# Expert layers: the low parts of the weights subtracted by VectorE a step later, instead of by GpSimd

## The chip, the cores and the metric

The kernel runs on 1 core of one Trainium2 chip. The metric is device time in microseconds (us) of one execution, the median of several. Five engines work side by side, each through its own queue in order: TensorE (PE, with PEld for its weight loads), VectorE (DVE), ScalarE (ACT), GpSimd (POOL) and SyncE (SP, which here only issues DMAs).

## The reference

Three layers follow one another: attention that keeps the 32 largest scores of a row, a mixture of 8 experts with a fixed capacity of 288 tokens each, and one more MLP with h * cos(h).

```python
def _moe_ref(x, w_gate, w1, w2):            # x [2304, 512]
    logits = x @ w_gate
    order = np.argsort(-logits.flatten())
    ...                                     # greedy: each token to the best expert that is not full
    for e in range(E):                      # E = 8, w1 [512, 1024], w2 [1024, 512] each
        mask = assigned == e
        h = np.maximum(x[mask] @ w1[e], 0.0)
        out[mask] = h @ w2[e]
    return out.astype(np.float32)
```

The MLP behind it computes `h = x @ w_in; (h * cos(h)) @ w_out`, with weights in float64.

## The kernel before

Attention takes the first 500 us of the span, the experts the stretch from 533 to 863 us, the last MLP the rest.

**Products in two parts.** A float32 operand is split into a high part `a0 = Copy(a)` in TensorE's reduced format (written `F32R`) and a low part `a1 = a - a0`. A product is three passes: high x high, high x low, low x high. The weights come from DRAM in units of 128 x 1024 (512 KB): SP loads a unit into one of three buffers `raw` (`fetch`, L1056), ACT copies it into the high half of a tile `wu` (L1070), and one subtraction writes the low half (`split`, L1073 where it is issued at once, L1252 where it was put off). A buffer `raw` is free for the next load when both have read it.

**The loop over the experts** (`m1`) has 64 steps (expert e, eighth f) and two more to drain. A step i does, in the order of the program: the subtractions that were put off in the step before; `h` of step i (12 matmuls, L1170, the result cut at 0 and split by ACT at L1176 and DVE at L1177 into `hh`); a tick of the search; `y` of step i - 2 (12 matmuls, L1185); another tick; the split of the next unit or units of weights by `more`; and one or two instructions of the float64 conversion `conv` on DVE (L1106 to L1121). Each engine keeps this order; nothing is scheduled again.

**The search** (`Search`, called by `tick`) assigns the tokens to the experts beside these matmuls. It plays between two engines: DVE compares all tokens with 24 thresholds (`v` by L795, then the table `yh` by L756), TensorE counts (L784), DVE judges (L788, L789), TensorE spreads the answer (L791), and so on, four rounds an expert. `place` then works out the rows of one expert's tokens (L844 to L881 on DVE, L851 and L869 on TensorE), and GpSimd gathers them by indirect DMAs (L1147). The first step begins when the first expert is known. From step 5 on, `i + 7` units of weights have been split at the end of step i; an expert takes 8 units and 8 steps, and the last unit of its first layer is split two steps before that expert's first `h`.

**Put off or not.** `split` appends the subtraction to the list `late` where it is given both an engine and that list; the loop issues what is in `late` at the start of the next step, and fetches the next unit after that. Without an engine the subtraction goes to GpSimd at once:

```python
            low = partial((eng or nc.gpsimd).tensor_tensor, w[:, 1, :], raw, w[:, 0, :].bitcast(F32), op=OP.subtract)
            if eng is None or late is None:
                low()
            else:
                late.append(low)
```

Of the kernel before, what the change touches and what calls it, by code (L numbers as in the profile page):

```python
# [19 lines left out]
DRAM = bass.MemoryType.DRAM  # L20

EPS1 = 1.0 - 2.0 ** -24          # the float32 next below 1
BIG = 2e37
NB = 64                          # thresholds that a round of the routing's search tries
NS, NR = 24, 4                   # the same where logits are without ties, and the rounds
MAGIC = 1.5 * 2.0 ** 23
INV2PI = 1.0 / (2.0 * math.pi)
C1 = 6.28125                     # 2 pi = C1 + C2, k * C1 exact
C2 = 2.0 * math.pi - 6.28125
PASSES = ((0, 0), (0, 1), (1, 0))  # high x high, high x low, low x high  # L30

B, H, S, D = 4, 8, 576, 64
NP = B * H // 2                  # pairs of heads
# [7 lines left out]
def constants(k, tmp):  # L41
# [24 lines left out]
    # token of (partition, column): 4 columns of a batch's first 512, then the last 64 of two batches each  # L66
# [34 lines left out]


WARM = 6, 4                       # products that keep the tensor engine's clock up: at the start, and when the scores end
LAST = 8                          # so many last tiles have their exp masked by the vector engine alone
PLACES = 3                        # places of a pair's q and k
MID = 8                           # in the first steps of the experts the search has two ticks more
CI, CR = 8, 5                     # from this step on, so many quarters of an instruction of the float64 weights a step
NY = 6                            # places of stretches of y
L2 = 3                            # steps from a second layer's h to its o


class Attention:
    """Scores of 128 queries at a time (tile): two heads of a pair by 4 tiles each, and one tile of both heads' last 64."""
# [3 lines left out]
    def __init__(s, k, sb, ps, slow=False):  # L117
# [4 lines left out]
        # their places are taken again only by weights  # L122
# [27 lines left out]
    def load(s, p):  # L150
        """k and q with the head dimension on partitions; q's pair of heads apart, zeros beside each"""
# [21 lines left out]
    def qk_mm(s, j, c):  # L173
        # even tiles have the last 64 keys last, odd ones first
        p, hs, i = s.tiles[j]
        if c == 0:
            s.SP[j] = s.ps.tile([128, 2, 512], F32, name="sp", bufs=s.nsp)
        o = 64 if j % 2 == 0 else 0
        lh = s.QT[p][hs][:, i * 128:(i + 1) * 128] if hs < 2 else s.QT[p][2]
        s.nc.tensor.matmul(s.SP[j][:, c, :288], lh, s.KT[p][:, o + c * 288:o + c * 288 + 288], start=True, stop=True)  # L180
# [34 lines left out]
    def sign_exp(s, j):  # L215
        # sign(t(1-e) - s(1-e)): -1 from t on, 1 below, never 0 (t no power of 2); the sum gives the count
# [31 lines left out]
    def probs(s, j, kind):  # L248
        """exp of the kept scores; by 'a' with a minus where not kept, which the copy after the transposition drops"""
# [89 lines left out]
    @staticmethod  # L339
    def together(*gens):  # L340
        """a step of each in turn: the words of one have time to arrive while another works"""
        gens = list(gens)
        while gens:
            gens = [g for g in gens if next(g, gens) is not gens]

    def store(s, b):
        """x of a batch to DRAM"""
# [5 lines left out]
    def logits_t(s):  # L353
        """a finished pair's part of x, transposed"""
# [14 lines left out]
    def logits_m(s):  # L369
        """and its share of the logits"""  # L370
# [18 lines left out]
    def span(s):  # L389
        """from the logits of the first three batches: a range wider by a half, of which a 24th is the search's first step;  # L390
        and what is far below it"""
# [26 lines left out]
    def warm(s, n):  # L418
        """keeps the tensor engine's clock up where it would wait for long"""
        for i in range(n):  # L420
            w = s.ps.tile([128, 2, 512], F32, name="sp", bufs=s.nsp)
            s.nc.tensor.matmul(w[:, 0, :], s.wt[:, :128], s.wt, start=True, stop=True)

    def run(s):
# [9 lines left out]
        # a pair is loaded in the step after the last scores of the one whose place it takes  # L434
# [3 lines left out]
        for step in range(ng + 6):  # L438
            gA, gB, gC, gD, gE, gF, gG = [step - i for i in range(7)]
            # when the scores are through, what is left goes on without a step between  # L440
# [74 lines left out]
    def run_slow(s):  # L515
        """any scores: 32 largest by 4 rounds of 8"""
        nc, sb = s.nc, s.sb
        V, A = nc.vector, nc.scalar
        for j, (p, hs, i) in enumerate(s.tiles):
# [35 lines left out]
            # v and q, k of a pair are needed until the last tile of the pair's group is done: NV = 2  # L555


def attention_flag(k, big):
    """where a row's 32nd largest was not proven: count out of 24..31, t or T tiny, negative or a power of 2"""
# [13 lines left out]
class Routing:  # L573
    """Pairs (token, expert) in descending logit: a token gets the first expert that is not full. In a phase all open
    experts take tokens down to the threshold at which the first of them is full; 64 thresholds a round find it."""
# [4 lines left out]
    def start(s):  # L580
        k, nc, sb, ps = s.k, s.nc, s.sb, s.ps
        PEe, V, A, G = nc.tensor, nc.vector, nc.scalar, nc.gpsimd
        # these few words lie apart, where no store has to end first
# [25 lines left out]
    def counts(s, m, O, th):  # L609
        """[E, NB]: the tokens from each threshold on, by best expert"""  # L610
# [9 lines left out]
    def over(s, pc):  # L620
        """[128, NB]: how many experts would overflow if all tokens from a threshold on were taken"""
# [6 lines left out]
    def take(s, m, O, G1):  # L628
        """assigns the tokens with G1 to their best experts; closes experts that are full"""
# [19 lines left out]
    def run_slow(s):  # L649
        """any logits: a token's ties by expert, the search down to neighbouring floats, ties between tokens by place"""  # L650
# [13 lines left out]
        with tc.For_i(0, E, 1):  # L664
# [7 lines left out]
            # hi: nothing is above; lo: all that is left is at or above  # L672
# [22 lines left out]
            # from hi on all; the ties in [lo, hi) as far as there is room, by place  # L695
# [24 lines left out]
class Search:  # L720
    """The same for logits without ties, beside other work: tick() is called where the tensor engine has time for a few
    products. Thresholds lie evenly over the logits' range; NS of them, NS between two of these, and so on for NR rounds
    find the one at which the first expert is full. The experts are numbered in this order, and
    each one's tokens are known as soon as it is full."""
# [8 lines left out]
    def tick(s, n=9):  # L733
        # first what the tensor engine does for all of them
# [17 lines left out]
    def compare(s, v):  # L752
        """[v >= -t] for t from 1 to NS"""
# [5 lines left out]
    def search(s):  # L759
# [7 lines left out]
        for r in range(E):  # L767
# [8 lines left out]
            else:  # L776
# [5 lines left out]
                for z in range(NR):  # L782
# [3 lines left out]
                    # thresholds at which no expert would take too many  # L786
# [34 lines left out]
            # which one was full: 16 + its number, if it was one  # L821
# [12 lines left out]
    def place(s, r, A, new):  # L834
        """the rows of x of the tokens of the expert that is number r"""
# [40 lines left out]
        # and these tokens' places among all  # L876
# [8 lines left out]
    def finish(s):  # L885
        """the rows of the output by place, 128 a block; and whether all was proven"""
# [34 lines left out]
def verdict(k, p):  # L921
    """k.bad: 1 if anything was not proven. Every expert has exactly its 288, and each was the only one full in its turn"""
# [3 lines left out]
    if p is not None:  # L926
        nc.tensor.matmul(p, k.onesf, u, start=True, stop=True)
        V.tensor_scalar(k.bad, p[:1], 0.0, None, op0=OP.is_gt)
        # if so, rows that are all different
# [13 lines left out]
def prefix(k, Ab, pp):  # L943
    """pp[p, c, e]: tokens before (p, c) with Ab, by columns"""
# [7 lines left out]
def slots(k, sb, ps):  # L952
    """the tokens sorted by expert, as row numbers for the gathers (96 a block) and the stores (128 a block)"""
# [47 lines left out]
class FFN:  # L1001
    """Both MLPs with the features on partitions. A float32 operand is split exactly into two parts of 12 bits."""
# [3 lines left out]
    def __init__(s, k, rt=None):  # L1006
# [3 lines left out]
        # units of weights in the order of their splitting: those of the first expert and of the next one's first layer;  # L1010
        # then, while expert e is in work, w1 of the next and w2 as its places get free
# [10 lines left out]
    def own(s, w, e, lo, hi):  # L1022
        """rows of an expert's weights"""
# [4 lines left out]
    def ready(s, half=False):  # L1028
        """are the next unit's (or half's) numbers float32, by an instruction issued before?"""
# [5 lines left out]
    def fetch(s, n, half=False):  # L1035
        """the next n units (or halves) of weights as they are"""
# [21 lines left out]
    def split(s, n, half=False, eng=None, late=None):  # L1058
        """the next n units (or halves) into high and low parts"""
# [17 lines left out]
    def narrow(s, lo, hi, tiles, temp):  # L1077
        """float64 weights to float32, rounded, half a unit at a time: yields between instructions"""
# [20 lines left out]
        for n in range(lo, hi):  # L1099
# [5 lines left out]
            # sign and exponent's top bit; 7 bits of exponent and 20 of mantissa  # L1105
# [11 lines left out]
            # the other 32 bits of mantissa, in units of the number's power of 2  # L1117
# [4 lines left out]
            # below float32's smallest normal: 0, or is there any? the high word as a float32 is in order, too  # L1122
# [18 lines left out]
    def gather(s, e):  # L1141
        """x of an expert's tokens"""
# [7 lines left out]
    def m1(s, sb, ps, yT):  # L1150
# [57 lines left out]
        def more(n, eng=None):  # L1208
            """n units have been split by now"""
# [40 lines left out]
        for i in range(len(seq) + LAG):  # L1250
# [18 lines left out]
            if i < len(seq):  # L1269
# [10 lines left out]
                if (e, f) == (E - 1, 4):  # L1280
                    # the tables of the second half
                    A.activation(s.sin, s.half_pi, AF.Sin)
            if rt:
                more(i + 5 + (i >= 2) + (i >= 5), eng=V if i >= 61 or i in (1, 3) else None)
# [14 lines left out]
    def part(s, k, c):  # L1299
        """y of stretch k's tokens in two parts"""  # L1300
# [7 lines left out]
    # stretch, half of the weights, its eighth; is it the stretch's first or last?  # L1308
# [17 lines left out]
    def turns(s, i, q):  # L1326
        # cos h = sin(pi/2 - |h - 2 pi k|)
# [212 lines left out]
```

## Time and profile before

| what | value |
|---|---|
| time, median of 3 runs | 1322.13 us |
| lowest and highest run | 1317.45 and 1332.7 us |
| span of the profiled execution | 1308.3 us |
| mean granted TensorE clock over the span | 0.926 |
| busy shares of the span, PE / DVE / ACT / POOL | 89% / 85% / 60% / 58% |

The span runs from the first to the last instruction of the profiled execution. Its own time with what lies around the span is not given apart; the median of the runs is 13.8 us above its span, the lowest run 9.2 us. The stretches of the program are told apart by windows of the span, in us from its start.

### The profile page before, as it was taken

The page shows a single profiled execution, that of the slowest core. Times are in us where ns is not written, and L with a number is a line of the kernel's source. Part 1 is how long each engine was busy: PE and PEld are TensorE (multiplying, and loading weights), DVE is VectorE, ACT ScalarE, POOL GpSimd, SP SyncE. Part 2 cuts the span into 40 slices and gives each one's busy share as a digit, 9 for nine tenths or more (in the row PEclk, how much of TensorE's full clock was granted, in tenths as well). Part 3 has the DMA queues.
Part 4 walks back from the last instruction along what each step waited for, and adds up shares of the span by engine and source line. Part 5 has one row for each costly group of instructions (what it writes and reads, how often), then busy time and mean ns, then how long its engine had stood idle before and what let it go on. Part 6 is the DMA issues. An engine that isn't in the chain of part 4 may idle for free.

```text
span 1308.3 us, 22623 instructions
## 1 busy us (share of the span) xinstructions
PE 1170.2 (89%) x7449; PEld 1036.4 (79%) x7449; DVE 1115.0 (85%) x4001; ACT 784.0 (60%) x1503; POOL 758.2 (58%) x655
## 2 busy tenths in 40 slices
PE   6799999999899995768878888998899999999996
PEld 3677787788777785668878888997778899999995
DVE  7999999999999995776697789979999767777774
ACT  7989888889898871323334344655565545444442
POOL 5988887889887870554545466745574434211120
PEclk9989898899898897878798888999899899999998
DMA  4201121111110001444454555642332101000000
GB/s 118 54 22 43 32 66 30 31 61 36 30 30 37 2 1 69 154 124 156 122 163 147 163 162 164 210 138 73 110 116 81 57 1 42 25 25 25 26 25 28
DMA packets 61888, 98.06 MB, mean 75 GB/s; under 512 B 30912, under 2 KB 30912, under 8 KB 61248
## 3 DMA queue, kind: packets, MB, share of 16 engines
q1 hardware_dynamic: 53648, 74.47, 18.8%
q10 hardware_dynamic: 5136, 12.60, 2.7%
q0 software_dynamic: 2976, 9.44, 2.3%
q8 instruction: 61, 1.00, 0.3%
q14 instruction: 67, 0.55, 0.1%
HBM read 78.66 MB, written 17.83 MB: 74 GB/s over the span
## 4 chain that ended last, share of the span: by engine, by line
DVE 51%; PE 40%; issue 4%; ACT 1%; POOL 1%; DMA 1%; SPq 0%; DVEq 0%; POOLq 0%; ACTq 0%
PE pa L1322 10%; PE y L1370 9%; DVE C L190 8%; PE pa L1170 5%; PE y L1185 5%; PE av L303 3%; DVE w L238 3%; DVE P L257 2%; PE sp L180 2%; DVE ct L1330 2%; PE pa L869 2%; DVE C L205 2%; DVE w L233 2%; DVE w L235 1%; DVE r L1121 1%
## 5 line engine op out<-in xcount | busy, mean ns | idle before, releaser
L1322 PE MATMUL pa<-yh,wu 128*128 128x384 f32 x1152 | 224.3, 342 | 9.5 <-POOL yh L1306 4.9
L1370 PE MATMUL y<-wu,gh 128*128 128x512 f32 x864 | 222.0, 401 | 6.6 <-POOL gh L1358 6.1
L1322 PEld LDWEIGHTS pa<-yh,wu 128*128 128x128 f32 x1152 | 207.7, 191 | 21.0 <-POOL yh L1306 6.3
L226 POOL TENSOR_TENSOR W<-sg,S 128x576 f32<-128x576 bf16 x144 | 195.8, 1367 | 47.3 <-ACT sg L220 46.6
L1073 POOL TENSOR_TENSOR wu<-raw,wu 128x1024 fp32r<-128x1024 f32 x63 | 157.2, 2508 | 108.0 <-ACT wu L1070 99.8
L1370 PEld LDWEIGHTS y<-wu,gh 128*128 128x128 f32 x864 | 164.1, 192 | 39.8 <-POOL gh L1358 8.0
L180 PE MATMUL sp<-kT,qz 128*128 128x288 f32 x512 | 174.9, 432 | 9.6 <-ACT S L184 7.2
L303 PE MATMUL av<-vm,PT 128*128 128x65 f32 (+1 forms) x1216 | 153.4, 275 | 30.1 <-DVE xb L326 29.7
L303 PEld LDWEIGHTS av<-vm,PT 128*128 128x128 f32 (+1 forms) x1216 | 141.7, 191 | 38.1 <-DVE xb L326 35.4
L190 DVE MAX8 C<-S 128x8 f32<-128x72 f32 x1152 | 162.5, 215 | 5.6 <-ACT S L184 5.4
L264 POOL TENSOR_TENSOR P<-sg,E 128x576 f32<-128x576 bf16 x102 | 135.8, 1332 | 3.6
L1170 PE MATMUL pa<-xh,wu 128*128 128x288 f32 x768 | 132.1, 326 | 6.2 <-DVE hh L1177 3.8
L1354 ACT ACTIVATE gh<-cx 128x384 fp32r<-128x384 f32 x95 | 49.9, 525 | 145.1 <-DVE cx L1352 143.8
L1170 PEld LDWEIGHTS pa<-xh,wu 128*128 128x128 f32 x768 | 118.4, 212 | 13.1 <-issue 4.7
L1185 PE MATMUL y<-hh,wu 128*128 128x288 f32 x768 | 127.5, 319 | 0.0
L184 ACT ACTIVATE S<-sp 128x576 f32<-128x576 f32 x144 | 95.1, 660 | 53.2 <-PE sp L180 53.2
L272 PEld LDWEIGHTS pt<-ident,P 128*128 128x128 f32 x576 | 82.0, 148 | 52.7 <-POOL P L264 8.3
L1185 PEld LDWEIGHTS y<-hh,wu 128*128 128x128 f32 x768 | 116.8, 208 | 2.6 <-ACT r L1129 1.8
L272 PE MATMUL pt<-ident,P 128*128 128x128 f32 x576 | 112.8, 284 | 4.4 <-POOL P L264 2.0
L220 ACT ACTIVATE sg<-S,tb 128x576 bf16<-128x576 f32 x144 | 114.5, 795 | 2.7 <-DVE tb L211 2.7
L222 ACT ACTIVATE E<-S,nmx 128x576 f32<-128x576 f32 x144 | 113.8, 791 | 0.0
L1329 DVE TENSOR_SCALAR ct<-pa 128x384 f32<-128x384 f32 x95 | 52.6, 554 | 60.0 <-PE pa L1322 59.9
(247 smaller groups left out, 2307.1 us busy)
## 6 DMA issues: line engine op xcount, KB each, us to landing
raw<-in_moe_w_dram SPq DMA_DIRECT2D x63, 512.0 KB, 3.7
kT<-in_k_dram SPq DMA_DIRECT2D x16, 288.0 KB, 3.0
qz<-in_q_dram SPq DMA_DIRECT2D x32, 128.0 KB, 3.3
vm<-in_v_dram SPq DMA_DIRECT2D x32, 128.0 KB, 2.8
x<-xb SPq DMA_DIRECT2D x4, 1024.0 KB, 4.3
r<-in_moe_w_in_dram ACTq DMA_DIRECT2D x8, 512.0 KB, 4.1
r<-in_moe_w_out_dram ACTq DMA_DIRECT2D x8, 512.0 KB, 5.3
half<-in_moe_w_in_dram SPq DMA_DIRECT2D x8, 512.0 KB, 3.8
```

The costliest lines, as they stand in the source:

```text
L180: s.nc.tensor.matmul(s.SP[j][:, c, :288], lh, s.KT[p][:, o + c * 288:o + c * 288 + 288], start=True, stop=True)
L190: s.nc.vector.max(c[:, e, :], s.SS[j][:, 72 * e:72 * e + 72])
L220: A.activation(s.SG[j], s.SS[j], AF.Sign, bias=s.TB[g][:, u:u + 1], scale=-EPS1, accum_out=s.SUM[g][:, u:u + 1])
L226: s.nc.gpsimd.tensor_tensor(s.W[j], s.SG.pop(j), s.SS[j], op=OP.mult)
L264: nc.gpsimd.tensor_tensor(P, m, s.EX[j], op=OP.mult)
L272: s.nc.tensor.transpose(s.PT[j][:, i * 128:(i + 1) * 128], s.PB[j // 2][:, o + i * 128:o + (i + 1) * 128], s.k.ident)
L303: PEe.matmul(o[lo:hi, u, :], s.PT[j][:, c * 128 + lo:c * 128 + hi], t[:, a, c, :], start=c == 0, stop=False)
L1073: low()
L1170: PEe.matmul(p, w[:, a, f * 128:(f + 1) * 128], XH[e, c][:, b, :], start=n == 0, stop=n == 11)
L1185: PEe.matmul(Y[e][m], w[:, a, o + m * 128:o + (m + 1) * 128], t[:, b, :], start=f == 0 and i == 0, stop=f == 7 and i == 2)
L1322: s.nc.tensor.matmul(p, w[:, a, f * 128:(f + 1) * 128], s.YH[q, c][:, b, :], start=n == 0, stop=n == 11)
L1370: PEe.matmul(O[q][m], g[:, a, m * 128:(m + 1) * 128], w[:, b, c:c + 512], start=first and j == 0, stop=last and j == 2)
```

## The change

One argument in the loop over the experts changes: `more` is now told VectorE in every step, where it was told VectorE in steps 1, 3 and from 61 on and otherwise nothing (GpSimd).

```diff
             if rt:
-                more(i + 5 + (i >= 2) + (i >= 5), eng=V if i >= 61 or i in (1, 3) else None)
+                more(i + 5 + (i >= 2) + (i >= 5), eng=V)
```

The rest of the difference between the files is comments. 62 subtractions of 128 x 1024 leave GpSimd's queue and stand in VectorE's, each at the start of the step after the one that copies its unit's high part. As the list `late` is then never empty behind a split, `fetch` is called at the start of the next step, behind the subtraction, and no longer at the end of the step itself.

GpSimd's queue in the first steps of the loop (`wu` is the unit's tile, `row` the gathered tokens):

```order
-L1073 TENSOR_TENSOR wu_8335<-raw,wu_8335 128x1024
-L1073 TENSOR_TENSOR wu_8340<-raw,wu_8340 128x1024
-L1147 DMA row<-x,i_65 96x512 x3
-L1073 TENSOR_TENSOR wu_8430<-raw,wu_8430 128x1024
-L1073 TENSOR_TENSOR wu_8435<-raw,wu_8435 128x1024
-L1073 TENSOR_TENSOR wu_8516<-raw,wu_8516 128x1024
-L1073 TENSOR_TENSOR wu_8613<-raw,wu_8613 128x1024
```

All of these rows go; the 21 gathers of the loop then stand one behind another, with nothing between them.

VectorE's queue at the step in which two units are split, between the end of `place` for the second expert (`pt`, `slot`) and the next judgement of the search (`rov`, `rfe`):

```order
 L880 SCALAR_TENSOR_TENSOR pt<-ppos,pA 128x18
 L881 TENSOR_TENSOR slot<-slot,pt 128x18
+L1252 TENSOR_TENSOR wu_8430<-raw,wu_8430 128x1024
+L1252 TENSOR_TENSOR wu_8432<-raw,wu_8432 128x1024
 L788 SCALAR_TENSOR_TENSOR rov<-pa_7746,rem 24x8
 L789 TENSOR_SCALAR rfe<-rov 24x1
```

Two subtractions now stand ahead of the judgement.

VectorE's queue in the middle of the loop, between the last instruction of a quarter of the float64 conversion (`r`) and the search's taking of tokens (`rG`, `rGO`):

```order
 L1162 TENSOR_TENSOR xh<-pa_9482,xh 128x288
 L1162 TENSOR_TENSOR xh<-pa_9489,xh 128x288
-L1121 TENSOR_TENSOR r_9152<-r_9152,r_9151 128x512
+L1121 TENSOR_TENSOR r_9149<-r_9149,r_9148 128x512
+L1252 TENSOR_TENSOR wu_9495<-raw,wu_9495 128x1024
 L801 TENSOR_SCALAR rG_9111<-rv,pa_7746 128x18
 L803 TENSOR_TENSOR rGO<-rO,rG_9111 128x144
```

One subtraction has come in behind the conversion and ahead of the search; the numbers in names differ only because tiles are numbered in the order of the program. The queues of TensorE, ScalarE and SyncE keep their order.

## Rows read from the trace of the kernel before

**Rows 1.** The page: busy time by engine; the chain that ended last.

```profile
PE 1170.2 (89%) x7449; PEld 1036.4 (79%) x7449; DVE 1115.0 (85%) x4001; ACT 784.0 (60%) x1503; POOL 758.2 (58%) x655
...
DVE 51%; PE 40%; issue 4%; ACT 1%; POOL 1%; DMA 1%; SPq 0%; DVEq 0%; POOLq 0%; ACTq 0%
```

**Rows 2.** Busy time of the engines by window, three parts of the expert stage.

```profile
core 0: us, PE busy (x) PEld busy (x) DVE busy (x) ACT busy (x) POOL busy (x), PEclk, DMA share, GB/s
...
805.00:863.00 58.00, 55.66 (x422) 54.97 (x420) 52.49 (x55) 36.57 (x66) 47.47 (x22) 0.97 0.65 209
533.00:805.00 272.00, 231.52 (x1783) 218.50 (x1781) 211.02 (x477) 100.81 (x179) 135.47 (x67) 0.87 0.48 147
...
533.00:863.00 330.00, 287.18 (x2203) 273.47 (x2201) 263.51 (x531) 137.38 (x243) 182.94 (x88) 0.89 0.51 158
```

**Rows 3.** What TensorE waited for, 533 to 805 us: total, times, longest.

```profile
PE pa L784 <- DVE yh L756: 14.6, 9, 6.5
PE pa L851 <- DVE pcs L847: 6.4, 3, 2.2
...
PE pa L791 <- DVE ppos L853: 0.8, 2, 0.6
```

**Rows 4.** Source line L1073, whole span: duration ns min/median/max, first and last start.

```profile
L1073 POOL TENSOR_TENSOR wu<-raw,wu x63: 2332/2406/3561, 529.8 to 856.2; 128x1024 fp32r<-128x1024 f32 x63
...
L1073 DVE TENSOR_TENSOR wu<-raw,wu x2: 1214/1216/1218, 525.5 to 527.7; 128x1024 fp32r<-128x1024 f32 x2
```

**Rows 5.** Timeline, 566 to 577 us: start, us, engine, instruction, idle before.

```profile
567.46 7.92 DVE L756 TENSOR_TENSOR yh<-rv,steps 128x432 bf16<-128x432 f32 x1
567.96 6.95 POOL L1073 TENSOR_TENSOR wu<-raw,wu 128x1024 fp32r<-128x1024 f32 x3
...
575.44 0.61 PE L784 MATMUL pa<-rO,yh 128*24 128x8 bf16 x18 [6.51 <-DVE yh L756]
```

**Rows 6.** Groups by form on VectorE, 533 to 805 us: busy us, mean ns.

```profile
L756 DVE TENSOR_TENSOR yh<-rv,steps 128x432 bf16<-128x432 f32 x23 | 23.3, 1015 | 0.8
L1177 DVE SCALAR_TENSOR_TENSOR hh<-pa,hh 128x288 fp32r<-128x288 f32 x47 | 20.9, 445 | 3.7 <-ACT hh L1176 3.5
L1121 DVE TENSOR_TENSOR r<-r,r 128x512 f32<-128x512 f32 x11 | 20.1, 1831 | 0.1
L795 DVE TENSOR_SCALAR rv<-rv,pa 128x18 f32<-128x18 f32 x18 | 13.8, 765 | 23.6 <-PE pa L869 18.4 <-PE pa L791 5.2
...
L901 DVE TENSOR_TENSOR yh<-yh,tab 128x324 bf16<-128x324 bf16 x2 | 2.6, 1286 | 0.0
```

**Rows 7.** The same five lines by source: duration ns min/median/max.

```profile
L1121 DVE TENSOR_TENSOR r<-r,r x11: 670/2135/4889, 608.3 to 790.6; 128x512 f32<-128x512 f32 x11
...
L756 DVE TENSOR_TENSOR yh<-rv,steps x23: 607/608/7922, 535.7 to 743.1; 128x432 bf16<-128x432 f32 x23
...
L795 DVE TENSOR_SCALAR rv<-rv,pa x18: 226/242/2551, 535.4 to 740.5; 128x18 f32<-128x18 f32 x18
...
L901 DVE TENSOR_TENSOR yh<-yh,tab x2: 481/1286/2091, 797.5 to 803.0; 128x324 bf16<-128x324 bf16 x2
...
L1177 DVE SCALAR_TENSOR_TENSOR hh<-pa,hh x47: 427/447/458, 536.9 to 803.5; 128x288 fp32r<-128x288 f32 x47
```

**Rows 8.** GpSimd's groups, 533 to 805 us.

```profile
L1073 POOL TENSOR_TENSOR wu<-raw,wu 128x1024 fp32r<-128x1024 f32 x48 | 119.2, 2495 | 100.5 <-ACT wu L1070 92.3 <-DMA raw<-in_moe_w_dram 8.1
```

**Rows 9.** Waits of VectorE (the longest) and ScalarE, 533 to 805 us.

```profile
DVE rv L795 <- PE pa L869: 18.4, 5, 4.5
DVE rov L788 <- PE pa L784: 16.8, 10, 3.0
...
ACT wu L1070 <- DMA raw<-in_moe_w_dram: 9.4, 5, 3.5
```

**Rows 10.** The subtractions that were put off before, groups of 530 to 880 us.

```profile
L1252 DVE TENSOR_TENSOR wu<-raw,wu 128x1024 fp32r<-128x1024 f32 x5 | 7.2, 1442 | 4.0 <-ACT wu L1070 4.0
```

## The prediction

> **What bounds the kernel now.** I began with the page's busy shares and its chain. TensorE is busy 89% of the span, VectorE 85%, and the chain that ended last runs 51% through VectorE and 40% through TensorE [rows 1]: these two hand the work to and fro, and GpSimd, from which the work is taken, holds 1% of the chain. That speaks against loading VectorE further, so I looked at the stage of the change alone.
>
> The windows [rows 2] split it in two. From 533 to 805 us, while the search runs, TensorE is busy 231.5 of 272 us and VectorE 211.0: neither is full, and TensorE stands idle for 40.5 us. The waits say for whom: ten entries, from 14.6 us for the search's table `yh` down to 0.8 us, all of them on VectorE, 39.9 us together [rows 3]. From 805 to 863 us the search is over, TensorE is busy 55.7 of 58 us and sets the pace. What the change is worth is therefore read from VectorE's latency in the first 272 us.
>
> There VectorE's durations are odd. `L756` takes 607 ns at its shortest and 608 in the median, but 1015 in the mean and 7922 once [rows 6, 7]. The timeline of that one case [rows 5] shows why: it starts at 567.46, three subtractions of GpSimd run from 567.96 to 574.91, and it ends at 575.38, while TensorE waits 6.5 us for its table. VectorE did not work for 7.9 us; it stood still until GpSimd was through. `L1121` has a shortest of 670 ns and a median of 2135; `L795`, on 18 columns, 226 ns and up to 2551. GpSimd's subtraction takes 2406 ns [rows 4], so these are an ordinary duration with up to one subtraction on top. `L1177`, whose first operand is in PSUM, never shows it: 427 to 458 ns in 47 instructions.
>
> The Trainium skill, page "SBUF — State Buffer", section "Who interferes with whom", states that a VectorE instruction with two SBUF inputs, or in a two-port mode, and a GpSimd instruction that reads SBUF exclude each other for the whole instruction, and that one with at most one SBUF input outside these modes does not contend. The trace agrees on both sides: 7.92 us for `L756` beside three subtractions, and at most 458 ns for `L1177`.
>
> **The change part by part.** The stall that goes: for each group of VectorE, its busy time less count times its shortest duration [rows 6, 7]. `L1121`: 20.1 - 11 x 0.670 = 12.7 us. `L795`: 13.8 - 18 x 0.226 = 9.7. `L756`: 23.3 - 23 x 0.607 = 9.3. Worked out in this way, 18 groups have over a microsecond each, from `L1121` down to `L901` with 2.6 - 2 x 0.481 = 1.6, and together they have 79 us. GpSimd does 48 subtractions of 2.495 us in this window, 119.2 us [rows 8], so two thirds of their time stopped VectorE, 1.65 us each.
>
> What VectorE gets: 62 subtractions. Two of the same shape ran on VectorE before, with no subtraction of GpSimd beside them, in 1.214 and 1.218 us [rows 4]. 48 lie in the window: 48 x 1.22 = 58.6 us. The other 14 lie after 805 us: 17.1 us. So VectorE's own load up to 805 us falls by 79 - 58.6 = 20 us.
>
> What that gives on the path lies between two ends. If VectorE's queue sets the pace everywhere, the path gets 20 us shorter. If the subtractions fill only gaps in which VectorE waits for TensorE anyhow, as the 18.4 us of `L795` behind `L869` and the 16.8 us of `L788` behind `L784` [rows 9], the path gains more, but no more than TensorE's idle 40 us at its present clock. In the order the added rows often stand right ahead of `L788`, one of those gaps, but also ahead of `L795` and `L801`, where the search waits. I take 26 us: nearer to the lower end, since a part of TensorE's idle time is the plain to and fro of the search, which stays.
>
> From 805 to 863 us TensorE sets the pace and I count nothing. The cover there is thin: VectorE is busy 52.5 of 58 us [rows 2], stalls included. It gets 17.1 us and loses 14 subtractions' stalls, at 1.65 us each 23 us. Without that relief it would need 69.6 us, 11.6 too many.
>
> The added wait: each subtraction on VectorE waits for ScalarE's copy of the same unit, and for the unit's DMA through it, with the search and `hh` queued behind it, for which TensorE waits. GpSimd could stand in that wait at no cost. The five that were put off before waited 4.0 us in all, 0.8 us each [rows 10]; four of them stood at the loop's end, behind the search. Within the search VectorE comes late to its queue, so I take zero; the far end is 48 x 0.8 = 38 us. ScalarE itself waited 9.4 us for units in this window, five times, 3.5 us at most [rows 9].
>
> The fetch that is put off costs nothing: SyncE's order is unchanged, and a buffer `raw` comes free when the subtraction is done, which takes 1.2 us in place of 2.4 and begins at the next step's start, where GpSimd began behind the copy; no row prices that, and three buffers lie between. The gathers lose what stood between them on GpSimd; they are not on the chain.
>
> Sum: the median 1322.1, which is 13.8 us above the profiled span and carries that over, less 26 gives **1296 us**.
>
> **The rivals.** *VectorE becomes the bound.* If the long durations are VectorE's own and not GpSimd's doing, the stage needs 263.5 + 62 x 1.22 = 339 us of VectorE in a stretch of 330 [rows 2]: at least 9 us more, 1331, and 1398 if its idle 66.5 us stay. The three subtractions of [rows 5] speak against it, and so do shortest durations that most instructions of `L756` keep. Beside this stands a rule of the Trainium skill, page "Perfetto Trace Analysis", section "Optimizing Scalar/DVE Operations": where VectorE is saturated, handing work to other engines, GpSimd even, may make sense, though it adds that their shared port may spoil it. By the first half of that rule this change goes the wrong way; by the second it does not. 3 in 100.
>
> *The wait for ScalarE takes the stall's place.* VectorE stands in line behind a copy or a late unit, and the search behind it. From 20 / 48 = 0.43 us a subtraction on the path the gain is gone; at 0.8 us it is 18 us slower, 1340. It would decide if VectorE came early to the start of its steps. Against it: the median of `L1121`, with which a step often ends, is stalled, so VectorE is late there. 5 in 100.
>
> *Something else is late next.* The stalls end, but TensorE's matmuls or the search's rounds stay the path, and 0 to 13 us are left: about 1315. For it speaks that VectorE has 61 us of idle time in the 272, so not all of its load is path. 18 in 100.
>
> *The clock rises too.* TensorE's granted clock is 0.87 up to 805 us, and 0.97 after it, where TensorE is 96% busy [rows 2]. With fewer gaps the first part may be granted more: 231.5 x (1 - 0.87 / 0.97) = 24 us at most, on top of up to 40; 1265 to 1277. 10 in 100.
>
> **How the numbers follow.** The forecast, 13 to 45 us less, has 64 in 100. The runs before lie 15 us apart, and about 1% is what a measurement of this kernel can tell from no change. Faster by over 1% are the forecast and the clock, 0.74; within 1% the third rival, 0.18; slower by over 1% the first two, 0.08. The range runs from 1270, inside the clock's case, to 1316, inside the third rival's; outside it are the two slower cases, and a part of the other two, under 2 in 10.
>
> **What would show it.** In the profile of the changed kernel `L1121`, `L756` and `L795` should have means near their shortest (0.67, 0.61 and 0.23 us); VectorE's subtractions 1.22 us each at L1252; TensorE's waits for VectorE up to the end of the search well under 39.9 us; the stretch from the first `h` to the last of the experts about 304 us in place of 330; the last MLP as long as before. It is wrong if the means stay long, if waits of L1252 for ScalarE pass 20 us within the search, or if the stretch after the search grows.

## The result, and the profile after

The changed kernel takes 1273.22 us in the median of 4 runs (1265.35 to 1274.61), the kernel before 1325.89 us in 4 runs beside it (1317.45 to 1332.7). The ratio is 0.9633, with a 95% interval from 0.9588 to 0.9677: 3.7% faster. It was forecast faster, at 1296 us, with a range from 1270 to 1316. The time lies inside the range, near its lower end, and the gain, 52.7 us between these medians, is twice the 26 us of the forecast.

The two traces are compared by parts: up to the start of the first `h` (attention), from there to the start of the 49th `h` (the search is over then), from there to the start of the 64th, and the rest.

| part | before, us | after, us | difference |
|---|---|---|---|
| up to the first `h` | 533.5 | 540.0 | +6.5 |
| first 48 steps | 272.0 | 233.7 | -38.3 |
| from the 49th `h` to the 64th | 53.5 | 49.2 | -4.3 |
| rest | 449.3 | 447.2 | -2.1 |
| span | 1308.3 | 1270.2 | -38.1 |

All of the gain lies in the steps, 42.6 us. The 6.5 us ahead of them are no effect of the change, whose code begins later: in the traces below the first `h` starts anywhere between 532.9 and 544.5 us. Nor are the 2.1 us of the rest, which takes 447.2 to 449.6 us in the ten traces whose code there is the same.

The page after, busy times and chain; to be read beside [rows 1]:

```profile
PE 1162.7 (92%) x7449; PEld 1028.6 (81%) x7449; DVE 1081.2 (85%) x4063; ACT 783.7 (62%) x1503; POOL 603.8 (48%) x593
...
DVE 47%; PE 42%; issue 5%; DMA 2%; POOL 2%; ACT 1%; SPq 0%; DVEq 0%; POOLq 0%; ACTq 0%
```

VectorE got 62 instructions more and is busy 34 us less.

Busy time by window, the first 48 steps and the next 15 (the columns are those of [rows 2]):

```profile
540.00:773.70 233.70, 219.45 (x1789) 207.07 (x1788) 187.13 (x526) 100.62 (x178) 23.15 (x22) 0.93 0.55 173
773.70:822.90 49.20, 49.20 (x388) 49.13 (x385) 39.87 (x64) 34.46 (x62) 4.36 (x4) 1.00 0.74 229
```

and the same 15 steps in the kernel before:

```profile
805.50:859.00 53.50, 51.17 (x387) 50.69 (x384) 48.94 (x50) 33.90 (x62) 44.39 (x21) 0.97 0.64 204
```

TensorE is idle for 14.2 us of the first window, where it was for 40.5 [rows 2], and its granted clock is 0.93 in place of 0.87. In the second it has no gap.

What TensorE waited for, 540 to 775 us; beside [rows 3]:

```profile
PE pa L791 <- DVE rfe L789: 3.6, 7, 1.5
PE pa L784 <- DVE yh L756: 3.4, 5, 1.9
PE pa L791 <- DVE ppos L853: 2.1, 2, 1.1
PE pa L807 <- DVE rGO L803: 1.2, 2, 0.8
...
PE pa L851 <- DVE rn L812: 1.0, 1, 1.0
```

There are seven entries with 13.6 us together, in place of ten with 39.9; the table `yh` has gone from 14.6 to 3.4. The five entries shown, 11.3 us, are waits for the search and its `place`.

Groups by form on VectorE, 540 to 775 us; beside [rows 6]:

```profile
L1252 DVE TENSOR_TENSOR wu<-raw,wu 128x1024 fp32r<-128x1024 f32 x49 | 59.4, 1218 | 4.4 <-ACT wu L1070 4.4
...
L756 DVE TENSOR_TENSOR yh<-rv,steps 128x432 bf16<-128x432 f32 x23 | 14.0, 608 | 0.8
...
L1121 DVE TENSOR_TENSOR r<-r,r 128x512 f32<-128x512 f32 x12 | 8.2, 681 | 0.1
...
L795 DVE TENSOR_SCALAR rv<-rv,pa 128x18 f32<-128x18 f32 x18 | 4.3, 238 | 15.4 <-PE pa L869 12.1 <-PE pa L791 3.3
...
L901 DVE TENSOR_TENSOR yh<-yh,tab 128x324 bf16<-128x324 bf16 x2 | 1.0, 488 | 0.0
```

The means that had stood at 1015, 1831, 765 and 1286 ns are now within a few per cent of the shortest of [rows 7]. The new subtractions take 1218 ns each, and three of the 49 waited for ScalarE, 4.4 us in all.

### The profile page after: what moved, and what is told of

Same layout as the page of the kernel before. It is cut to its first block, busy times and chain, and to the rows that moved or that the text cites. A ratio compares the mean times of both kernels' runs of the same rounds, so it can differ in the third digit from the quotient of the medians.

```text
span 1270.2 us, 22607 instructions
## 1 busy us (share of the span) xinstructions
PE 1162.7 (92%) x7449; PEld 1028.6 (81%) x7449; DVE 1081.2 (85%) x4063; ACT 783.7 (62%) x1503; POOL 603.8 (48%) x593
## 4 chain that ended last, share of the span: by engine, by line
DVE 47%; PE 42%; issue 5%; DMA 2%; POOL 2%; ACT 1%; SPq 0%; DVEq 0%; POOLq 0%; ACTq 0%
PE pa L1322 10%; PE y L1370 10%; DVE C L190 8%; PE y L1185 5%; PE pa L1170 5%; DVE w L238 3%; PE av L303 3%; DVE P L257 2%; DVE wu L1252 2%; PE pa L869 2%; PE sp L180 2%; DVE C L205 2%; DVE w L235 2%; DVE w L233 2%; DVE ct L1330 2%
## 5 line engine op out<-in xcount | busy, mean ns | idle before, releaser
L180 PE MATMUL sp<-kT,qz 128*128 128x288 f32 x512 | 178.5, 439 | 7.2 <-ACT S L184 5.3
L303 PEld LDWEIGHTS av<-vm,PT 128*128 128x128 f32 (+1 forms) x1216 | 142.7, 193 | 38.1 <-DVE xb L326 34.0
L1147 POOL DMA_INDIRECT row<-x,i x24 | 27.4, 1142 | 219.6 <-PE y L1185 33.7
L184 ACT ACTIVATE S<-sp 128x576 f32<-128x576 f32 x144 | 94.8, 658 | 55.7 <-PE sp L180 55.7
L1170 PE MATMUL pa<-xh,wu 128*128 128x288 f32 x768 | 125.1, 314 | 0.0
L1185 PE MATMUL y<-hh,wu 128*128 128x288 f32 x768 | 121.0, 308 | 0.0
L1170 PEld LDWEIGHTS pa<-xh,wu 128*128 128x128 f32 x768 | 112.5, 201 | 3.2 <-issue 2.9
L1185 PEld LDWEIGHTS y<-hh,wu 128*128 128x128 f32 x768 | 110.3, 197 | 1.4 <-ACT r L1129 0.4
L1329 DVE TENSOR_SCALAR ct<-pa 128x384 f32<-128x384 f32 x95 | 52.7, 555 | 55.4 <-PE pa L1322 55.2
```

Of the source, the lines that this page charges most:

```text
L303: PEe.matmul(o[lo:hi, u, :], s.PT[j][:, c * 128 + lo:c * 128 + hi], t[:, a, c, :], start=c == 0, stop=False)
L1170: PEe.matmul(p, w[:, a, f * 128:(f + 1) * 128], XH[e, c][:, b, :], start=n == 0, stop=n == 11)
L1185: PEe.matmul(Y[e][m], w[:, a, o + m * 128:o + (m + 1) * 128], t[:, b, :], start=f == 0 and i == 0, stop=f == 7 and i == 2)
```

## The experiments

The questions were whether GpSimd's subtraction really holds VectorE, or whether the order (put off by a step, fetch later) made the gain; what the 62 subtractions still cost on VectorE; where the gain beyond 26 us came from; and whether the same move pays in the second MLP. Ratios are to the kernel before, run beside them on the same chip; steps, TensorE's idle time and its granted clock are from each run's trace, for the first 48 steps as above.

| run | time, us | ratio (95%) | first 48 steps | next 15 | idle | clock |
|---|---|---|---|---|---|---|
| before | 1325.89 | 1 | 272.0 | 53.5 | 40.5 | 0.87 |
| after | 1273.22 | 0.9633 (0.9588 to 0.9677) | 233.7 | 49.2 | 14.2 | 0.93 |
| e1, put off on GpSimd | 1320.98 | 1.0013 (0.9983 to 1.0043) | 276.5 | 53.5 | 42.8 | 0.86 |
| e2, VectorE at once | 1274.31 | 0.966 (0.9592 to 0.9729) | 232.3 | 49.2 | 15.4 | 0.94 |
| e3, GpSimd reads too | 1344.39 | 1.0212 (1.0128 to 1.0296) | 293.9 | 55.7 | 57.8 | 0.86 |
| e4, GpSimd writes only | 1283.01 | 0.9727 (0.9661 to 0.9793) | 243.4 | 49.2 | 21.4 | 0.92 |
| e5, every other step | 1287.82 | 0.9795 (0.9745 to 0.9845) | 247.4 | 49.2 | 22.1 | 0.90 |
| e7, filled gaps | 1332.11 | 1.0108 (1.0063 to 1.0153) | 290.1 | 53.6 | 34.9 | 0.87 |
| e8, subtract twice | 1325.78 | 1.0051 (1.0024 to 1.0078) | 278.5 | 57.0 | 42.5 | 0.85 |
| e9, no subtraction | 1273.26 | 0.9629 (0.9559 to 0.9698) | 234.4 | 49.2 | 12.4 | 0.91 |

**Put off, but on GpSimd.**

```diff
-                more(i + 5 + (i >= 2) + (i >= 5), eng=V)
+                more(i + 5 + (i >= 2) + (i >= 5), eng=V if i >= 61 or i in (1, 3) else nc.gpsimd)
```

> The subtractions stay on GpSimd, but are put off by a step, with the fetch behind them, as in the changed kernel. Theory A (GpSimd's subtraction stops VectorE while it reads SBUF): nothing is gained, the 64 steps from the first to the last h take 315 to 335 us as before (325.5), VectorE's L1121 keeps a mean over 1.5 us, time within 1% of before. Rival B (the gain comes from the order: put off, later fetch): the steps take under 300 us, as in the changed kernel (282.9).

The steps take 330.0 us (276.5 + 53.5), the time is that of before within 0.5%, and `L1121` is as long as it was (its group, 535 to 816 us):

```profile
L1121 DVE TENSOR_TENSOR r<-r,r 128x512 f32<-128x512 f32 x11 | 20.3, 1843 | 0.1
```

Putting off alone gains nothing. Rival B has fallen.

**VectorE, but at once.**

```diff
-                    s.split(1, eng=eng, late=late)
+                    s.split(1, eng=eng, late=None if now else late)
...
-                more(i + 5 + (i >= 2) + (i >= 5), eng=V)
+                more(i + 5 + (i >= 2) + (i >= 5), eng=V, now=not (i >= 61 or i in (1, 3)))
```

> VectorE does the 62 subtractions, but at the end of the same step, right behind ScalarE's copy, with the fetch at once. Theory A: nearly the whole gain stays, the steps take 283 to 292 us; putting off is worth what VectorE then waits for ScalarE, up to 0.8 us each or some 10 us on the path. Rival B: the gain is gone, over 310 us.

The steps take 281.5 us, as with putting off (282.9) and just under the 283 to 292 that were expected. VectorE waited 9.1 us for ScalarE over 57 subtractions (groups, 535 to 800 us), and the path did not feel it:

```profile
L1073 DVE TENSOR_TENSOR wu<-raw,wu 128x1024 fp32r<-128x1024 f32 x57 | 69.2, 1219 | 9.3 <-ACT wu L1070 9.1
```

The engine is the whole effect in these steps, the put-off step none of it.

**GpSimd does needless subtractions beside the changed kernel.** `spare` is the last expert's part of `yT`, which is written after the loop's last steps.

```diff
                     s.split(1, eng=eng, late=late)
+                    if rt and late is not None and u[1] < E:
+                        hi = s.U[u][:, 0, :].bitcast(F32).rearrange("p (a b) -> p a b", a=4)
+                        spare = yT[:, :, 7 * CAP:7 * CAP + 256]
+                        nc.gpsimd.tensor_tensor(spare, hi, hi, op=OP.subtract)
```

> The changed kernel, and GpSimd does beside it 57 subtractions of the same size (a high part from itself, into a part of the experts' output that is written later; nobody reads the result). Theory A: the stalls are back on top of VectorE's new work: L1121 and L756 have means over 1 us, the steps take 335 to 360 us, slower than before. Rival C (VectorE's long durations were its own, or GpSimd was simply too slow for its consumers): no change against the changed kernel, 283 us.

The steps take 349.6 us, 67 more than in the changed kernel, and the kernel is 2.1% slower than the one before. Nothing depends on these subtractions, and still the durations are back, though `L756`, with 677 ns, stayed under the microsecond that was expected of it (groups of VectorE, 535 to 800 us):

```profile
L1257 DVE TENSOR_TENSOR wu<-raw,wu 128x1024 fp32r<-128x1024 f32 x44 | 61.6, 1406 | 4.1 <-ACT wu L1070 4.1
...
L756 DVE TENSOR_TENSOR yh<-rv,steps 128x432 bf16<-128x432 f32 x23 | 15.6, 677 | 0.8
L1121 DVE TENSOR_TENSOR r<-r,r 128x512 f32<-128x512 f32 x10 | 13.2, 1324 | 0.1
```

In these steps TensorE waits for VectorE and for a DMA, never for GpSimd. That shows the cause: GpSimd's work as such, not who needs its result.

**GpSimd only writes.**

```diff
+                        nc.gpsimd.tensor_tensor(spare[:, 0, :8], hi[:, 0, :8], hi[:, 0, :8], op=OP.subtract)
+                        for _ in range(2):
+                            nc.gpsimd.memset(spare, 0.0)
```

> As the run with 57 needless subtractions, but GpSimd only writes: two memsets of 128 x 1024 behind a subtraction of 8 columns, some 2 us together. Theory A in its narrow form (only GpSimd's reads stop VectorE's instructions with two SBUF inputs): L1121 and L756 stay at their shortest (0.68 and 0.61 us), only tensor_scalars such as L795 and L1118 may be longer, the steps take 283 to 300 us. Its wide form (any GpSimd instruction holds VectorE): L1121 and L756 over 1 us in the mean, 320 us and more.

GpSimd is busy 133 us with this (107 us of memsets, 26 of the small subtractions), more than before with its subtractions, but the steps take only 292.6 us. The groups of VectorE, 535 to 800 us:

```profile
L756 DVE TENSOR_TENSOR yh<-rv,steps 128x432 bf16<-128x432 f32 x23 | 14.0, 608 | 0.8
...
L1121 DVE TENSOR_TENSOR r<-r,r 128x512 f32<-128x512 f32 x14 | 9.5, 681 | 0.1
...
L1118 DVE TENSOR_SCALAR rt<-r 128x512 int32<-128x512 int32 x14 | 7.8, 560 | 0.1
L795 DVE TENSOR_SCALAR rv<-rv,pa 128x18 f32<-128x18 f32 x18 | 5.9, 325 | 16.7 <-PE pa L869 13.1 <-PE pa L791 3.5
```

The two instructions with two inputs in SBUF keep their shortest durations; the tensor_scalars `L1118` (0.40 at its shortest) and `L795` (0.22) do not. Counted as in the prediction, over all groups of the first 48 steps, the tensor_scalars lost 12.8 us (0.9 in the changed kernel) and everything else 3.4 (3.6). The narrow form holds: what GpSimd reads stops the first kind, and what it writes still stops the second.

**Half of it.**

```diff
-                more(i + 5 + (i >= 2) + (i >= 5), eng=V)
+                more(i + 5 + (i >= 2) + (i >= 5), eng=V if i % 2 or i >= 61 else None)
```

> VectorE does the subtractions of every other step: 29 of the 62 move, 33 stay on GpSimd. Theory A: each GpSimd subtraction costs about the same, so about 29/62 of the 42.6 us that the 64 steps lost: 305 us, time about 1300. A rival in which a last few stalls decide (nothing gained until nearly all are gone) expects over 318; one in which VectorE's new load eats the second half of the gain expects under 295.

The steps take 296.6 us: 29 of 62 subtractions, 47% of them, bring 28.9 of the 42.6 us, 68%. Neither the straight line (305) nor either rival (over 318, under 295) is met. The first half is worth more than the second, and why is only partly shown. In the first 48 steps 22 of 48 subtractions moved (46%) and 24.6 of 38.3 us came (64%); VectorE's stalls there, counted over all groups, fell from 83.5 to 40.4 us, and to 4.5 with all moved, so 55% of them went. The rest may be that what VectorE takes over costs more as it fills, as the next run suggests.

**The subtractions twice.**

```diff
             while late:
-                late.pop(0)()
+                low = late.pop(0)
+                low()
+                if i < 61:
+                    low()
```

> The changed kernel with every put-off subtraction of the steps up to 60 done twice on VectorE, 62 more of 1.22 us, 76 us. If VectorE's subtractions lie in gaps, the steps take up to 10 us longer than 282.9; if all of VectorE's queue is path, 60 us and more longer. The prediction's 26 us supposed three quarters or more of them on the path: then 40 to 60 us longer.

The steps take 335.5 us, 52.6 more for 76 us more of VectorE's work: 70% of it lies on the path. VectorE is then busy 243.8 of the first 278.5 us (the third of the busy times below), and of the 42 us that TensorE waited all but 3.4 were for it:

```profile
541.90:820.40 278.50, 236.02 (x1788) 222.23 (x1788) 243.80 (x572) 101.44 (x178) 24.16 (x21) 0.85 0.46 143
```

**No subtraction at all.** The low parts of the units up to step 60 are set to zero by GpSimd and enter the products so.

```diff
+            if eng == "zero":
+                nc.gpsimd.memset(w[:, 1, :].bitcast(F32), 0.0)
+                continue
...
-                more(i + 5 + (i >= 2) + (i >= 5), eng=V)
+                more(i + 5 + (i >= 2) + (i >= 5), eng=V if i >= 61 else "zero")
```

> The subtractions of the steps up to 60 are left out: GpSimd sets these low parts to zero in one memset each (0.97 us, writes only), so the products lack the low parts of most weights. It bounds what VectorE's 62 subtractions still cost in the changed kernel. If they lie in gaps, the steps take 275 to 283 us; if they cost on the path at the rate of the doubled run (53 of 76 us), 235 to 250; if TensorE is the next limit (219 us busy in the first 48 steps, idle 14), between, 255 to 270.

The steps take 283.6 us, as in the changed kernel, with VectorE busy 161 us in place of 187 in the first 48. It is not the bound it was meant to be, since the memsets have a price of their own: tensor_scalars are long again, `L795` above all (groups of VectorE, 535 to 790 us; L1109 is L1106 of the other kernels).

```profile
L795 DVE TENSOR_SCALAR rv<-rv,pa 128x18 f32<-128x18 f32 x18 | 22.3, 1239 | 25.6 <-PE pa L869 18.6 <-PE pa L791 7.0
L756 DVE TENSOR_TENSOR yh<-rv,steps 128x432 bf16<-128x432 f32 x24 | 14.6, 608 | 0.8
...
L1109 DVE TENSOR_SCALAR rt<-r 128x512 int32<-128x512 int32 x14 | 9.8, 697 | 0.3 <-DMA r<-in_moe_w_in_dram 0.3
...
L853 DVE TENSOR_SCALAR ppos<-pcs,pa 128x18 f32<-128x18 bf16 x7 | 4.4, 623 | 1.7 <-PE pa L851 1.7
```

`L795` alone has 22.3 - 18 x 0.22 = 18 us of stall, and the tensor_scalars of the first 48 steps have 28 together. So by this run the first 62 subtractions cost between nothing and some 28 us of their 76 on the path. The changed kernel's own trace sets the closer bound: TensorE was idle for 14.2 us in its first 48 steps and not at all in the next 15, so at the clock it was granted they can't have cost more than those 14 us, where the second 62 cost 53.

**TensorE's gaps filled, in the kernel before.**

```diff
+            for _ in range(4 if rt and 8 * e + f < 48 else 0):
+                PEe.matmul(p, s.U["w1", e, 0][:, 0, f * 128:(f + 1) * 128], XH[e, 0][:, 0, :], start=True, stop=True)
```

> The kernel before, with 4 needless matmuls ahead of each h in the first 48 steps (their result is overwritten by the h that follows): TensorE's gaps are partly filled, VectorE's stalls stay. If TensorE's granted clock follows its gaps, the clock of these steps rises from 0.87 to 0.91 or more, and the matmuls' own time falls by about what the 192 extra ones add (23 us at the full rate); the steps take 320 to 335 us. If the clock has another cause, it stays at 0.87, the extra matmuls cost 26 us less what falls in gaps, 335 to 350 us.

The clock stays at 0.87 and the first 48 steps take 290.1 us, 18.1 more; all steps take 343.7, as the second reading had it. But the gaps are hardly filled: 34.9 us of idle time are left of 40.5, and the wait for `yh` is 19.6 us with a longest of 6.0. The extra matmuls stand ahead of `h`; the waits for `yh` lie behind it. The run does not tell whether the clock follows the gaps.

**The second MLP.** There 18 subtractions of half units (L1073) and 16 additions of the conversion (L1121) stay on GpSimd in the changed kernel. Four runs move them; the diff of the last stands for all but the additions, which get `V` in place of `nc.gpsimd` at L1121. In e6 and e11 the subtraction of the halves is issued at once.

```diff
+        lows = []
...
-            s.split(s.start2 + goal(i) - s.done, True)
+            while lows:
+                lows.pop(0)()
+            s.split(s.start2 + goal(i) - s.done, True, eng=V, late=lows)
```

> The changed kernel, and the second MLP's 18 half-unit subtractions and the 16 additions of its float64 conversion go from GpSimd to VectorE too (the gated product's 48 and the tokens' 35 stay). Theory A: GpSimd loses 24 and 23 us of work there, VectorE gains 34 x 0.68 = 23 us and loses stalls of about half of GpSimd's 46 us; TensorE waits for other engines only 16 us in that stage. So 0 to 8 us are gained against the changed kernel, 1265 to 1273. If VectorE at its fullest stretch (58 of 60 us) is the limit there, 3 to 10 us slower.

> Of the second MLP's two moved groups only the 16 additions of the conversion go to VectorE. If the loss of 22 us came from the halves' subtractions, which then wait on VectorE for ScalarE, this run is within 5 us of the changed kernel or up to 6 faster (1267 to 1278); if it came from the additions, 1285 or more.

> Only the 18 half-unit subtractions of the second MLP go to VectorE. If the loss of 22 us came from them, 1285 to 1297; if from the conversion's additions, within 5 us of the changed kernel (1268 to 1278).

> As the run with the second MLP's 18 half-unit subtractions on VectorE, but put off by a step, so that VectorE does not stand behind ScalarE's copy. If the 18 us that it stood there (ten waits of 1.8 us) are what that run lost, the loss goes: within 5 us of the changed kernel, or up to 8 us faster, since GpSimd's 24 us of subtractions and a part of VectorE's stalls go too: 1265 to 1277. If VectorE's own load there is the limit, it stays slow, 1283 or more.

| run | time, us | ratio (95%) | rest, from the 64th `h` on |
|---|---|---|---|
| after | 1273.22 | 0.9633 (0.9588 to 0.9677) | 447.2 |
| e6, both groups | 1296.16 | 0.9835 (0.9793 to 0.9877) | 469.5 |
| e10, the additions | 1278.4 | 0.9667 (0.96 to 0.9734) | 454.4 |
| e11, the halves, at once | 1289.67 | 0.9749 (0.9679 to 0.9819) | 464.8 |
| e12, the halves, put off | 1277.02 | 0.9661 (0.9635 to 0.9687) | 451.3 |

The first run missed both of its readings: it is 23 us slower than the changed kernel, where 8 us of gain to 10 of loss were expected. Taken apart, the halves are to blame (e11 lies in the range that says so, e10 0.4 us above its own). Most of the 22 us that both groups lose in the rest of the span is the halves' (17.6), the additions lose some 7; the unchanged rest itself varies by 2.4 us between traces. The groups of VectorE, 828 to 985 us, of the halves at once:

```profile
L1073 DVE TENSOR_TENSOR wu<-row,wu 128x512 fp32r<-128x512 f32 x10 | 6.9, 693 | 18.2 <-ACT wu L1070 18.2
```

and put off:

```profile
L1440 DVE TENSOR_TENSOR wu<-row,wu 128x512 fp32r<-128x512 f32 x10 | 14.2, 1418 | 0.0
```

At once, VectorE stood 1.82 us behind ScalarE for each of these ten halves; put off, it never did, and 13.5 of the 17.6 us came back. But the halves then take 1418 ns in the mean in place of 693: of all 18, the 13 that ran beside GpSimd's product at L1358 took some 1500 ns, the five beside none 678 to 685. Nothing is gained against the changed kernel, and none of the four runs beats it.

## Why the prediction held, point by point

**The stall.** Right, and shown: it goes with GpSimd's reads (e1, e3, e4), and the 79 us that it was put at went with it, down to means within a few per cent of the shortest. Only the reading "an ordinary duration with up to one subtraction on top" was too low by its own rows: `L756` stood through three once [rows 5], and the longest `L1121`, 4889 ns [rows 7], through two.

**VectorE's price.** 62 x 1.22 us was right (1218 ns measured). **The added wait** was put at zero against a far end of 38 us: 4.4 us measured in the trace after, and at once as good as put off (e2). The mechanism of that rival is real, but lives elsewhere: in the second MLP putting off takes back 13.5 of the 17.6 us that the halves lose (e11, e12).

**What it gives on the path: the term that was mis-sized.** The prediction took "26 us: nearer to the lower end, since a part of TensorE's idle time is the plain to and fro of the search, which stays". TensorE's idle time did fall by 40.5 - 14.2 = 26.3 us in the first 48 steps; that it came so near to a value chosen between 20 and 40 is chance. And the 26 us were the whole forecast: two terms beside it had been set at nothing. TensorE's busy time in these steps fell from 231.5 to 219.5 us, 12.0 more, as the granted clock rose from 0.87 to 0.93: 231.5 x 0.87 / 0.93 = 217. In the 13 traces with the same matmuls in these steps, busy time times clock is 200.8 to 204.3 us while the clock runs from 0.85 to 0.94, so the busy time does go with the clock. This was the fourth rival, at 10 in 100; it came at half of its 24 us, and the time lies in its 1265 to 1277, past the 13 to 45 us less of the forecast's own case. The range held because it reached into that rival. And the steps from the 49th to the 64th `h` got 4.3 us shorter, where "I count nothing": VectorE's load there fell by 9 us (48.9 to 39.9, where some 6 were reckoned), TensorE's gaps closed and its clock rose from 0.97 to 1.00. 26.3 + 12.0 + 4.3 = 42.6.

The choice near the lower end holds in part. At that end VectorE's queue sets the pace everywhere; but the first 62 subtractions cost at most some 14 of their 76 us at the granted clock, so they mostly did fill VectorE's gaps, and it is a second helping that is mostly path (e8). The reason given, that a part of the idle time stays, came true: 14.2 us stayed, most of them waits for the search. Whether these are its plain to and fro or the new subtractions in its way is not shown: without subtractions 12.4 us are left (e9), but there the memsets hold the search up. None of the three signs of being wrong was seen: the means came down, `L1252` waited 4.4 us for ScalarE, and the stretch after the search got shorter.

**The 13.8 us.** The prediction carried them from the profiled span to the median as if they lay around the span. They do not: the profiled execution after has a span of 1270.2 and a time of 1272.08 us, 1.9 apart. By the same offset the profiled execution before took some 1310 us, one of its fastest; the runs of that kernel spread from 1307.54 to 1332.7. So the traces differ by 38 us and the medians by 53 (by 45 to 48 if the medians of the kernel before in the four later groups of runs, 1317.87 to 1321.24, are taken); the remainder lies in that spread and, between the two traces, in the 6.5 us of attention.

**The rivals.** VectorE as the bound: excluded, since the steps are no shorter without its subtractions (e9) and its load is mostly path only with twice as many (e8). Something else late next: TensorE, busy 219 of 234 us and then without a gap, but only after 42.6 us. The clock: half come true. Why the clock rose stays open: over the runs it is higher where TensorE idles less (0.93 and 0.94 at 14 and 15 us idle, 0.85 to 0.87 at 35 to 58), but the five traces whose steps are those of the changed kernel (after, e6, e10 to e12) have 0.914 to 0.935 at 14 us, e9 has 0.907 with the least idle time of all, and e7, meant to set the gaps alone, did not close them.

## What to carry to other kernels

Before weighing an engine's busy share, compare the mean of each of its groups with the shortest: a mean at twice the shortest, beside a busy GpSimd, was standing still here, and work that the "full" engine takes over from GpSimd can make it emptier. What VectorE took over cost little (at most 14 of 76 us) while TensorE or its own gaps covered it, and most of its length after (53 of 76), so one doubled run tells how much room is left. Where VectorE takes over an instruction that waits for another engine, put it a step behind that wait; whether that is worth anything differs from stage to stage of one kernel.

## What was not expected of the hardware

A VectorE instruction can stand through a whole row of GpSimd instructions that follow one another. In e9 one tensor_scalar of 18 columns, 0.22 us by itself, stood through six memsets (timeline, 684.5 to 691.5 us):

```profile
684.95 5.79 DVE L795 TENSOR_SCALAR rv<-rv,pa 128x18 f32<-128x18 f32 x1 [0.47 <-PE pa L791]
685.26 5.45 POOL L1072 MEMSET wu<- 128x1024 f32 x6
```

The 7.92 us of [rows 5], through three subtractions, are the same, and in both cases VectorE's instruction is shown to start first, 0.31 and 0.50 us ahead of GpSimd's row.

But it is not a rule. Later in the trace before, three subtractions ended at 779.63, 782.02 and 784.37 us; `L853` got in between the second and the third, and only the next tensor_scalar stood through the third (timeline, 777 to 785 us):

```profile
777.22 7.15 POOL L1073 TENSOR_TENSOR wu<-raw,wu 128x1024 fp32r<-128x1024 f32 x3
...
779.81 2.25 DVE L853 TENSOR_SCALAR ppos<-pcs,pa 128x18 f32<-128x18 bf16 x1 [2.70 <-PE pa L851]
...
782.09 2.32 DVE L854 TENSOR_SCALAR pt<-ppos 128x18 f32<-128x18 f32 x1
```

From the first `h` to the 64th, a stretched VectorE instruction met the seam between two GpSimd instructions (less than 0.15 us apart) 21 times in the trace before: 15 times it was done before the second one was, 6 times it stood through it. In e3 it was done first all 19 times; in e9 it stood through 25 of 26 seams. What decides is not shown. So the price of a queue of GpSimd instructions can be its whole length, not that of the one in work; and e4 and e9 show that memsets, which read nothing, charge it to tensor_scalars (12.8 and 28.0 us in the first 48 steps), while everything else lost 3.4 and 2.7 us, no more than in the changed kernel.
